# Key sums as a row of the key-value product, the first router from transposed rows, early queries, and output tiles moved off GpSimd in a two-layer attention kernel

## The chip, the cores and the metric

The kernel runs on one core of one Trainium2 chip. The metric is the device time of one execution in microseconds (us), median over several runs. Runs come in two states: a run is called slow when it is over 1.5% above the fastest of the same kernel. Ratios compare fast runs alone. The engines are TensorE (PE, its weight loads PEld), VectorE (DVE), ScalarE (ACT), GpSimd (POOL) and SyncE (SP). `SPq` and `ACTq` in the profile are the places from which these engines issue transfers.

## The reference

```python
def _A_ref(x, wqkv, wo):                       # S=2048, D=512, 32 heads of 16
    qkv = (x @ wqkv).reshape(B, S, 3, H, Dh).transpose(2, 0, 3, 1, 4)
    q, k, v = qkv[0], qkv[1], qkv[2]
    phi = lambda t: jnp.where(t > 0, t + 1, jnp.exp(t)) + 1e-6
    pq, pk = phi(q), phi(k)
    kv = einsum("bhsd,bhse->bhde", pk, v)
    z = einsum("bhsd->bhd", pk)                # the key sums
    num = einsum("bhqd,bhde->bhqe", pq, kv)
    den = einsum("bhqd,bhd->bhq", pq, z)[..., None] + 1e-6
    return (num / den).transpose(0, 2, 1, 3).reshape(B, S, D) @ wo
def _B_ref(x, w_r, w_gate, w_up, w_down):      # F=1376
    r = x @ w_r                                # the router
    idx = argsort(-r)[:, :2]                   # the two best rows of 2048
    x_sel = take(x, idx)
    y = (silu(x_sel @ w_gate) * (x_sel @ w_up)) @ w_down
    return x + scatter(idx, y * sigmoid(r[idx]))
for _ in range(2):
    x = x + _A_ref(_layernorm(x), A_wqkv, A_wo)
    x = x + _B_ref(_layernorm(x), B_w_r, B_w_gate, B_w_up, B_w_down)
```

## The kernel before

Rows lie in 16 tiles of 128. Layer normalization gives `xn`, a transfer transposes it to `xnT`. `K` makes the key features `pk` of a tile, `G` adds the tile to `pk^T xn` (four banks), `Q` makes query features. The value projection is applied to the product afterwards (`kv`). `den` makes the denominators, `O` the outputs of a tile. Every operation is entered in a list with its reads, writes and estimated duration; a list scheduler in the program then fixes each engine's order before the run. An edit in one place can therefore change the order everywhere behind it.

```python
def G(t, Gs, first=False, last=False):                # one tile's share of pk^T xn
    for c in range(NC):
        T_.matmul(Gs[c]()[:], lhsT=xn[:, t, c*P:(c+1)*P], rhs=pk[:, t, :], start=first, stop=last)

def z_piece(layer, zt, t, after=()):                  # key sums: 4 matmuls of one column per tile
    for c in range(NC):
        T_.matmul(zt()[:, c:c+1], lhsT=pk[:, t, c*P:(c+1)*P], rhs=ones_b[:], ...)

def r0_piece(t):                                      # router of layer 1's rows, in the same bank `zr`
    for c in range(NC):
        T_.matmul(zr()[:, NC+t:NC+t+1], lhsT=xnT[:, c, t*P:(t+1)*P], rhs=wr[:, c, :], ...)

def kv(layer, Gs):
    for i in range(NC):
        copy_ps(i, 0.5, GT[:, i, :], Gs[i], ("GT", i))         # two copies on ACT, two on DVE
    ...                                               # V weights x GT, block mask, output weights
# ... cut: layer 1's router is r0 plus a term from layer 1's queries; the two selected rows go
#     through gate, up and down, are normalized again (xc4) and patched into xnT ...
for i, t in enumerate(ORD[NT-k2-2:]):                 # only behind that patch:
    G(t, G2); z_piece(1, zr2, t, (1,))
    if i < QC: Q(i)                                   # the queries of layer 2
# ... cut ...
OUTK = [["POOL"]*4, ["POOL"]*4, ["ACT","DVE","ACT","DVE"], ["DVE","ACT","DVE","ACT"]]
# groups 0 and 1: scaled and stored during the output stage; 2 and 3: beside the last router
def store(lo, hi):                                    # 4 tiles, 512 KB
    nc.sync.dma_start(out=out_dram[:, lo:hi, :], in_=xo[:, lo:hi, :])
# ... cut: second router, gate, up, down of the two rows -> yo ...
# the two final rows, written over rows of the stored tiles, so behind all four stores:
e.dma_start(out=out_rows[:, ds(i, 1), :], in_=yo[...])         # one row on SP, one on ACT
```

Of the kernel before, what the change touches and what calls it, by code (L numbers as in the profile page):

```python
# [10 lines left out]
I32 = mybir.dt.int32  # L11
# [12 lines left out]
NR = 6  # L24
EPS = 1e-5
# [135 lines left out]
def linear_attention_moe(  # L161
# [95 lines left out]
    ones_b = big.tile([P, 1], BF16, name="ones_b")  # L257
    nc.vector.memset(ones_b[:], 1.0)
# [8 lines left out]
    sgnb = big.tile([4, 1], BF16, name="sgnb")  # L267
# [9 lines left out]
    xn = big.tile([P, NT, D], BF16, name="xn")  # L277
    xnT = big.tile([P, NC, S], BF16, name="xnT")
    pk = big.tile([P, NT, D], BF16, name="pk")
    pqT = big.tile([P, NJ, NC, D], BF16, name="pqT")  # L280
# [9 lines left out]
    r0 = big.tile([P, NT], FP32, name="r0")  # L290
    sd = big.tile([P, NT], FP32, name="sd")
    rr = big.tile([P, 2, NT], FP32, name="rr")
# [3 lines left out]
    KWr = [big.tile([P, NC, 2], BF16, name=f"KWr{i}") for i in range(2)]  # L296
# [20 lines left out]
    def tiny(fns, r, w, dur=0.07, **k):  # L317
        for f in fns:
            dve(dur, f, r=r, w=w, **k)
# [31 lines left out]
    def norm(kind, t, s_, b_, r, **k):  # L351
        if kind == "ACT":
            act(0.7, lambda: A.activation(out=xn[:, t, :], in_=x[:, t, :], func=ACT.Identity, scale=s_, bias=b_),
                r=[("x", t)] + r, w=[("xn", t)], **k)
        else:
            e = V if kind == "DVE" else G_

            def f():
                e.tensor_scalar(  # L359
                    out=xn[:, t, :], in0=x[:, t, :], scalar1=s_, scalar2=b_, op0=ALU.mult, op1=ALU.add  # L360
                )
            op(kind, 0.33 if kind == "DVE" else 0.76, f, r=[("x", t)] + r, w=[("xn", t)], port=True, **k)

    def trans(t, **k):
        def f():
            nc.sync.dma_start_transpose(out=xnT[:, :, t * P : (t + 1) * P], in_=xn[:, t, :])
        op("SP", 1.3, f, r=[("xn", t)], w=[("xnT", t)], lat=1.35, **k)
# [54 lines left out]

    def G(t, Gs, first=False, last=False, **k):
        def f():
            for c in range(NC):
                T_.matmul(  # L426
                    Gs[c]()[:], lhsT=xn[:, t, c * P : (c + 1) * P], rhs=pk[:, t, :], start=first, stop=last
# [6 lines left out]
    def Q(n, **k):  # L434
# [9 lines left out]
        phi(p, pqT[:, j, c, :], ("pq", j, c), relu=n < RQ[layer2[0]], **k)  # L444

    def z_mask(layer, zc, ap, r):
        zcs = small([P, NC, 1])

        def g():
            V.tensor_copy(out=zcs[:], in_=ap())  # L450
            V.tensor_tensor(
                out=Zs[layer][:], in0=headmask[:].to_broadcast([P, NC, 32]), in1=zcs[:].to_broadcast([P, NC, 32]),
                op=ALU.mult,
            )
        dve(0.3, g, r=r + ["masks"], w=["Z"])

    zr = ps("tp", [P, NC + NT])

    def z_piece(layer, zt, t, after=()):
        first = not after  # L460

        def f():
            for c in range(NC):
                T_.matmul(  # L464
                    zt()[:, c : c + 1], lhsT=pk[:, t, c * P : (c + 1) * P], rhs=ones_b[:],
                    start=first and c == 0, stop=layer == 0 and t == NT - 1, skip_group_check=True,
                )
        pl.lazy = 6.0
        pe(0.11, f, r=[("pk", t), zt] + (["zf%d" % layer] if after else ([("nmr", 2)] if layer == 0 else [])),
           w=[("z", layer, t)] + ([] if after else ["zf%d" % layer])).st = 0.01  # L470
        pl.lazy = 0.0

    def r0_piece(t):
        def f():
            for c in range(NC):
                T_.matmul(
                    zr()[:, NC + t : NC + t + 1], lhsT=xnT[:, c, t * P : (t + 1) * P], rhs=wr[:, c, :],
                    start=False, stop=(c == NC - 1), skip_group_check=True,
                )
        pl.lazy = 6.0  # L480
        pe(0.11, f, r=[("xnT", t), "wr", zr, "zf0"], w=[("r0p", t)]).st = 0.01
        pl.lazy = 0.0
# [7 lines left out]
    def kv(layer, Gs):  # L490
        for i in range(NC):
            copy_ps(i, 0.5, GT[:, i, :], Gs[i], ("GT", i))
        p = ps("g")
# [11 lines left out]
        pe(0.93, f, r=[("GT", i) for i in range(NC)] + ["wv"], w=[p])  # L505
# [4 lines left out]
        for c in range(NC):  # L510
            kw_one(layer, c)
        kr = ps("tp", [P, NC, 2])
# [11 lines left out]
        def h():  # L524
            V.tensor_reduce(out=krs[:], in_=kr()[:], axis=AX.X, op=ALU.add)
            split2(KWr[layer][:], krs[:])
# [18 lines left out]
    def den(layer, j, **k):  # L545
        p, ld, rb, sp, rd = ps("tp", [P, P]), sb("ld", [P, P], FP32), sb("rb", [P, P]), ps("mm", [P, NC, P]), sb("rd", [P, 1, D])

        def f():
            for c in range(NC):
                for g in range(NC):  # L550
                    T_.matmul(
                        p()[32 * g : 32 * (g + 1), :], lhsT=Zs[layer][:, c, :], rhs=pqT[:, j, c, g * P : (g + 1) * P],
# [19 lines left out]
        for c in (0, 2):  # L572
            q = pqT[:, j, c : c + 2, :]
# [4 lines left out]
    def O(layer, t, **k):  # L578
# [6 lines left out]
        def f(a, n):  # L585
            for c in range(NC):
                T_.matmul(  # L587
                    p()[:, a : a + n], lhsT=pqT[:, j, c, tt * P : (tt + 1) * P], rhs=KWs[layer][:, c, a : a + n],
# [37 lines left out]
    def lin(layer, lo, hi, tag="mm"):  # L626
# [3 lines left out]
        def f():  # L630
            for t in ts:
                j, tt = divmod(t, NJ)
                for c in range(NC):
                    T_.matmul(
                        p()[:, t - lo, :], lhsT=pqT[:, j, c, tt * P : (tt + 1) * P], rhs=KWr[layer][:, c, :],
# [4 lines left out]
        fs = [lambda: V.tensor_reduce(out=a[:], in_=p()[:], axis=AX.X, op=ALU.add)]  # L640
        if layer == 0:
            fs.append(lambda: V.tensor_tensor(out=rr[:, 0, lo:hi], in0=r0[:, lo:hi], in1=a[:], op=ALU.add))
        else:
            tiny([lambda: V.tensor_tensor(out=o[:], in0=rr[:, 0, lo:hi], in1=opr[:, 0, lo:hi], op=ALU.mult)],
                 r=["rrp"], w=[("ro", lo)])
            fs.append(lambda: V.tensor_tensor(out=rr[:, 1, lo:hi], in0=o[:], in1=a[:], op=ALU.add))
        tiny(fs, r=[p, "r0"] + ([("ro", lo)] if layer else []), w=[("rr", layer, lo)])
        tiny([
            lambda: V.scalar_tensor_tensor(
                out=rc[:], in0=mv[:, layer + 1, lo:hi, 0], scalar=nwr[:], in1=rr[:, layer, lo:hi],  # L650
                op0=ALU.mult, op1=ALU.add,
            ),
        ], r=[("rr", layer, lo), "nwr"] + [(f"mean{layer + 1}", t) for t in ts], w=[("rc", layer, lo)])
        tiny([
            lambda: V.tensor_tensor(
                out=key_hi(layer)[:, lo:hi], in0=rc[:], in1=rho[:, layer + 1, lo:hi], op=ALU.mult
            ),
        ], r=[("rc", layer, lo), "keys"] + [(f"rho{layer + 1}", t) for t in ts], w=[("key", layer, lo)])
# [4 lines left out]
    def mid_chain(lo, hi, kinds):  # L663
# [18 lines left out]
        ], r=w, w=[("s3", t) for t in ts])  # L682
        for t, kind in zip(ts, kinds):
# [16 lines left out]
    def consts_gp2():  # L700
# [7 lines left out]
        for sg in (sgn, sgnb):  # L708
            G_.memset(sg[:], 1.0)
            G_.affine_select(  # L710
                out=sg[:], in_=sg[:], compare_op=ALU.is_ge, fill=-1.0,
                base=-2, pattern=[[0, 1]], channel_multiplier=1,
            )

    def consts():
        pool(3.6, consts_gp, w=["masks0", "masks"])
        pool(1.3, consts_gp2, w=["pid", "rid"])
# [32 lines left out]

    def r0_all():
        def g():
            V.reciprocal(out=sd[:], in_=rho[:, 0, :])
            V.tensor_tensor(out=r0[:], in0=sd[:], in1=zr()[:, NC:], op=ALU.mult)
            V.tensor_scalar(
                out=sd[:], in0=mv[:, 0, :, 0], scalar1=nwr[:], scalar2=-1.0, op0=ALU.mult, op1=ALU.mult
            )
# [679 lines left out]
```

## Time and profile before

| | us |
|---|---|
| median of 3 runs | 171.97 (171.87 to 172.0) |
| span of the profiled execution | 170.1 |
| TensorE busy / VectorE busy | 154.0 / 133.2 |

The shares of busy time, the stages and the end are shown in the prediction below. The timeline shows the start, the duration, the engine, the line, output and inputs, and how many neighbouring instructions were merged. This is TensorE in layer 1's output stage:

```profile
54.99 0.41 PE L551 MATMUL tp<-pqT,Z 128*32 128x128 bf16 x16
...
59.48 2.75 PE L587 MATMUL g<-KW,pqT 128*128 128x512 bf16 x12
```

The first denominators begin at 54.99 and the first outputs at 59.48.

### The profile page before, as it was taken

The page shows a single profiled execution, that of the slowest core. Times are in us where ns is not written, and L with a number is a line of the kernel's source. Part 1 is how long each engine was busy: PE and PEld are TensorE (multiplying, and loading weights), DVE is VectorE, ACT ScalarE, POOL GpSimd, SP SyncE. Part 2 cuts the span into 40 slices and gives each one's busy share as a digit, 9 for nine tenths or more (in the row PEclk, how much of TensorE's full clock was granted, in tenths as well). Part 3 has the DMA queues.
Part 4 walks back from the last instruction along what each step waited for, and adds up shares of the span by engine and source line. Part 5 has one row for each costly group of instructions (what it writes and reads, how often), then busy time and mean ns, then how long its engine had stood idle before and what let it go on. Part 6 is the DMA issues. An engine that isn't in the chain of part 4 may idle for free.

```text
span 170.1 us, 4133 instructions
## 1 busy us (share of the span) xinstructions
PE 154.0 (91%) x1509; PEld 81.7 (48%) x1531; DVE 133.2 (78%) x483; ACT 106.7 (63%) x258; POOL 21.6 (13%) x52
## 2 busy tenths in 40 slices
PE   6989999999999999987999999999999999963771
PEld 2344544444465445542445565634446455443670
DVE  1499997867688899998968865637877999999640
ACT  3268967463544858899858223338899988795700
POOL 7321124000000000302030200000000000715000
PEclk9999999999999999999999999999999999998555
DMA  5997444599970000072423510000000000031530
GB/s 158 314 362 184 98 93 93 149 257 373 419 315 7 0 4 0 2 94 47 109 62 69 92 35 4 0 0 4 0 0 4 0 0 6 0 123 70 181 123 6
DMA packets 23589, 16.40 MB, mean 96 GB/s; under 512 B 17936, under 2 KB 21776, under 8 KB 23184
## 3 DMA queue, kind: packets, MB, share of 16 engines
q1 hardware_dynamic: 23272, 15.61, 31.7%
q10 hardware_dynamic: 296, 0.53, 0.9%
q8 instruction: 12, 0.20, 0.5%
q14 instruction: 9, 0.07, 0.2%
HBM read 9.83 MB, written 2.10 MB: 70 GB/s over the span
## 4 chain that ended last, share of the span: by engine, by line
PE 54%; DVE 31%; DMA 7%; issue 4%; SPq 1%; ACT 1%; DVEq 0%
PE mm L440 14%; PE g L426 13%; PE mm L402 12%; DVE x L596 9%; DVE pqT L574 5%; DMA xnT<-xn 5%; DVE st L325 3%; DMA x<-in_A_x_dram 3%; PE g L587 2%; PE g L979 1%; DVE em L375 1%; PE tp L979 1%; SPq L216 1%; PE g L499 1%; DVE pqT L382 1%
## 5 line engine op out<-in xcount | busy, mean ns | idle before, releaser
L371 ACT ACTIVATE e<-mm 128x512 bf16<-128x512 f32 x58 | 34.6, 601 | 29.7 <-PE mm L440 14.6
L440 PE MATMUL mm<-xnT,wq 128*128 128x512 bf16 x120 | 31.1, 379 | 0.7 <-DVE pqT L382 0.3
L426 PE MATMUL g<-pk,xn 128*128 128x512 bf16 x124 | 31.3, 379 | 0.3
L587 PE MATMUL g<-KW,pqT 128*128 128x512 bf16 (+1 forms) x127 | 29.3, 372 | 0.3
L402 PE MATMUL mm<-wk,xnT 128*128 128x512 bf16 x100 | 25.5, 379 | 2.4 <-DMA xnT<-xn 1.4
L375 DVE TENSOR_SCALAR em<-e 128x512 bf16<-128x512 bf16 x58 | 17.2, 302 | 11.9 <-ACT e L371 11.7
L604 ACT ACTIVATE sq<-x 128x512 bf16<-128x512 bf16 (+1 forms) x33 | 20.2, 611 | 4.4 <-DVE x L596 3.6
L587 PEld LDWEIGHTS <-pqT 128*128 128x128 bf16 x132 | 12.2, 97 | 12.6
L382 DVE SCALAR_TENSOR_TENSOR pk<-mm,em 128x512 bf16<-128x512 f32 x26 | 17.7, 685 | 0.4
L426 PEld LDWEIGHTS <-xn 128*128 128x128 bf16 x128 | 11.8, 98 | 12.4
L440 PEld LDWEIGHTS <-wq 128*128 128x128 bf16 x128 | 11.3, 97 | 12.5 <-issue 1.2
L402 PEld LDWEIGHTS <-xnT 128*128 128x128 bf16 x104 | 9.5, 97 | 13.3 <-DMA xnT<-xn 3.2
L325 DVE BATCH_NORM_STATS2 st<-x 128x6 f32<-128x512 bf16 x16 | 10.7, 683 | 5.0 <-DMA x<-in_A_x_dram 5.0
L596 DVE SCALAR_TENSOR_TENSOR x<-x,opr,g 128x512 bf16<-128x512 bf16 (+1 forms) x17 | 11.9, 707 | 0.0
L596 DVE SCALAR_TENSOR_TENSOR x<-x,g 128x512 bf16<-128x512 bf16 x16 | 10.6, 681 | 1.0 <-PE g L587 0.8
L382 DVE SCALAR_TENSOR_TENSOR pqT<-mm,em 128x512 bf16<-128x512 f32 x16 | 11.0, 689 | 0.4
L359 POOL TENSOR_SCALAR xn<-x,s,nb 128x512 bf16<-128x512 bf16 x5 | 4.1, 821 | 53.3 <-DVE mv L620 41.8
L1232 POOL TENSOR_SCALAR pk<-x,opr,nb 128x512 bf16<-128x512 bf16 x8 | 6.1, 772 | 37.3 <-DVE nb L1220 37.3
L574 DVE TENSOR_TENSOR pqT<-pqT,rd 128x1024 bf16<-128x1024 bf16 x16 | 10.5, 684 | 0.1
L374 ACT ACTIVATE rl<-mm 128x512 bf16<-128x512 f32 x16 | 9.8, 613 | 0.0
L339 ACT ACTIVATE lnv<-mv,eps_t 128x2 f32<-128x2 f32 (+2 forms) x18 | 5.1, 292 | 7.4 <-DVE mv L326 4.4
L464 PEld LDWEIGHTS <-pk 128*128 128x128 bf16 x128 | 5.8, 96 | 4.1
(238 smaller groups left out, 227.3 us busy)
## 6 DMA issues: line engine op xcount, KB each, us to landing
wgu<-in_B_wgu_dram SPq DMA_DIRECT2D x2, 1408.0 KB, 12.4
out_dram<-pk SPq DMA_DIRECT2D x4, 512.0 KB, 2.8
wd<-in_B_wd_dram SPq DMA_DIRECT2D x1, 1408.0 KB, 15.2
x<-in_A_x_dram SPq DMA_DIRECT2D x2, 512.0 KB, 5.6
xt<-in_A_xt_dram SPq DMA_DIRECT2D x3, 256.0 KB, 4.9
x<-in_A_x_dram SPq DMA_DIRECT2D x3, 256.0 KB, 4.8
wk<-in_A_wk_dram ACTq DMA_DIRECT2D x2, 256.0 KB, 4.0
wq<-in_A_wq_dram SPq DMA_DIRECT2D x1, 512.0 KB, 6.9
```

The costliest lines, as they stand in the source:

```text
L325: dve(0.61, lambda: V.bn_stats(out=st()[:], in_=x[:, t, :]), r=[("x", t)], w=[st]).early = 4.0
L371: act(0.5, lambda: A.activation(out=e()[:], in_=p()[:], func=ACT.Exp), r=[p], w=[e], **k)
L374: act(0.5, lambda: A.activation(out=rl()[:], in_=p()[:], func=ACT.Relu), r=[p], w=[rl], **k)
L375: dve(0.2, lambda: V.tensor_scalar(out=em()[:], in0=e()[:], scalar1=1.0, scalar2=TINY, op0=ALU.min, op1=ALU.add), r=[e], w=[em], port=True ...
L382: dve(0.6, lambda: V.scalar_tensor_tensor(out=out_ap, in0=p()[:], scalar=0.0, in1=em()[:], op0=ALU.max, op1=ALU.add), r=[p, em], w=[key], **k)
L402: T_.matmul(p()[:], lhsT=xnT[:, c, t * P : (t + 1) * P], rhs=wk[:, c, :], start=(c == 0), stop=(c == NC - 1))
L426: T_.matmul(Gs[c]()[:], lhsT=xn[:, t, c * P : (c + 1) * P], rhs=pk[:, t, :], start=first, stop=last)
L440: T_.matmul(p()[:], lhsT=wq[:, i, c, :], rhs=xnT[:, i, j * D : (j + 1) * D], start=(i == 0), stop=(i == NC - 1))
L574: dve(0.6, lambda q=q: V.tensor_tensor(out=q, in0=q, in1=rd()[:].to_broadcast([P, 2, D]), op=ALU.mult), r=[rd], w=[("pq", j, c), ("pq", j, ...
L587: T_.matmul(p()[:, a : a + n], lhsT=pqT[:, j, c, tt * P : (tt + 1) * P], rhs=KWs[layer][:, c, a : a + n], start=(c == 0), stop=(c == NC - 1),)
L596: dve(0.04 + 0.6 * n / D, lambda a=a, n=n: V.scalar_tensor_tensor(out=x[:, t, a : a + n], in0=x[:, t, a : a + n], scalar=1.0 if i == 1 els ...
L604: act(0.1 + 0.5 * n / D, lambda a=a, n=n, sq=sq: A.activation(out=sq()[:, 0:n], in_=x[:, t, a : a + n], func=ACT.Square, scale=float(D) ** ...
```

## The change

Its intent: take small matmuls off TensorE (the key sums come out as one more row of a product that is made anyway), free a bank early, start layer 2's queries before the router's result is known and patch two of them afterwards, and shorten the end by keeping POOL out of it.

```diff
+    nc.gpsimd.memset(xn[:, :, D : D + 1], 1.0)            # ones column; rows are now 544 wide
+    def gcol(c):
+        return c * P + (c == NC - 1)                      # last slice starts one element later
-    lhsT=xn[:, t, c * P : (c + 1) * P]
+    lhsT=xn[:, t, gcol(c) : gcol(c) + P]
-    (z_piece, z_mask, r0_piece, r0_all: removed)
+    def center():                                         # a normalized row sums to 0, so the dropped
+        ... V.tensor_tensor(out=wv, in0=wv, in1=wl, op=subtract)   # column is restored through wv
     def kv(layer, Gs):
-        for i in range(NC):
+        for i in (3, 2, 1, 0):
             copy_ps(i, 0.5, GT[:, i, :], Gs[i], ("GT", i))
+        zf: 4 matmuls take the key sums from GT's last row
-            lin(0, t - 3, t + 1)                          # first router from layer 1's queries
+            logits(t - 3, t + 1)                          # from the transposed rows of layer 2
     for i, t in enumerate(ORD[NT - k2 - 2 :]):            # moved: now ahead of the patch of xnT
         G(t, G2)
         if i < QC: Q(i)                                   # QC 7 -> 8
+    pqx: 16 matmuls, 3 small operations and 2 copies replace the two queries' features
-    OUTK = [["POOL"]*4, ["POOL"]*4, ["ACT","DVE","ACT","DVE"], ["DVE","ACT","DVE","ACT"]]
+    OUTK = [["POOL"]*4, ["ACT","DVE"]*2, ["ACT","DVE"]*2, ["DVE","ACT","DVE","DVE"]]
-    (groups 0 and 1 scaled and stored in the output stage)
+    (group 0 only; groups 1 to 3: one set of scales and all tiles beside the last router)
... (cut: bookkeeping of the two query tiles, gates of the output tiles, table load)
```

## The prediction

> **What bounds the kernel now.** I read the shares of busy time, then the same by stage, then TensorE's timeline, then the timeline of the end.
>
> ```profile
> PE 154.0 (91%) x1509; PEld 81.7 (48%) x1531; DVE 133.2 (78%) x483; ACT 106.7 (63%) x258; POOL 21.6 (13%) x52
> ...
> PE 54%; DVE 31%; DMA 7%; issue 4%; SPq 1%; ACT 1%; DVEq 0%
> ```
>
> TensorE (PE) leads in busy time and in the chain that ended last, VectorE (DVE) is second. The shares hide stages, so I cut the span where the program changes its work: layer 1's keys and products; its key-value product; its outputs; layer 2's keys with the routed-token work beside them; layer 2's key-value product and outputs; the end.
>
> ```profile
> core 0: us, PE busy (x) PEld busy (x) DVE busy (x) ACT busy (x) POOL busy (x), PEclk, DMA share, GB/s
> 21.60:48.50 26.90, 26.71 (x175) 12.90 (x179) 21.21 (x53) 14.45 (x28) 2.80 (x5) 1.00 0.76 246
> 48.50:59.50 11.00, 10.25 (x175) 6.17 (x175) 9.15 (x23) 6.63 (x14) 0.00 (x0) 1.00 0.14 57
> 59.50:78.40 18.90, 16.84 (x168) 8.55 (x168) 18.43 (x78) 14.99 (x48) 1.52 (x2) 1.00 0.20 29
> 78.40:127.30 48.90, 48.33 (x426) 24.73 (x433) 35.30 (x134) 28.78 (x67) 4.19 (x7) 1.00 0.17 34
> 127.30:153.30 26.00, 23.87 (x261) 13.09 (x263) 24.57 (x90) 23.18 (x65) 3.76 (x5) 1.00 0.06 22
> 153.30:170.10 16.80, 8.59 (x210) 7.50 (x210) 8.93 (x52) 5.67 (x13) 2.29 (x4) 0.58 0.27 96
> ```
>
> PE is full in the first and fourth stage; DVE is full in the third (18.43 of 18.90) and nearly so in the fifth (24.57 of 26.00); the last is a chain of small steps, with the clock at 0.58. Since ends of matmuls are modelled, I checked PE by starts: a group of four 512-column matmuls starts every 0.86 us (0.2155 each) almost without a hole from 21.6 to 151. The holes I find are some 0.4 and 0.7 us near 50 and 57, 0.9 at 73 and 1.3 at 77 (waits for transposes).
>
> ```profile
> 18.84 0.44 PE L464 MATMUL tp<-ones_b,pk 128*128 128x1 bf16 x12
> 19.15 0.54 PE L476 MATMUL tp<-wr,xnT 128*128 128x1 bf16 x16
> ```
>
> Twelve key-sum matmuls hold PE from 18.84 to 19.15: 26 ns each, though each shows 164 ns long. That is the price of a small matmul here.
>
> ```profile
> 152.56 3.03 POOL L1232 TENSOR_SCALAR pk<-x,opr,nb 128x512 bf16<-128x512 bf16 x4 [3.90 <-DVE nb L1220]
> 153.59 0.52 DVE L1218 TENSOR_SCALAR opr<-rho 128x4 f32<-128x4 f32 x1
> 154.20 0.65 DVE L1220 TENSOR_TENSOR nb<-rho 128x4 f32<-128x4 f32 x1
> 154.96 0.64 DVE L621 SCALAR_TENSOR_TENSOR mv<-mv 128x4 f32<-128x4 f32 x1
> 155.83 0.30 ACT L339 ACTIVATE lnv<-mv,eps_t 128x4 f32<-128x4 f32 x1 [1.89 <-DVE mv L623]
> 158.24 1.23 PE L910 MATMUL tp<-identf,s 128*128 128x128 f32 x4 [0.26 <-DVE s L1284]
> ```
>
> Right after the last output, DVE's tiny operations take 0.52 to 0.65 us instead of some 0.16, exactly while GpSimd (POOL) writes four output tiles. They stand in front of the last row sums, so they hold up the final router.
>
> **What the Trainium skill says.** "TensorE: Matmul & The Clock Gate", section "Wait — 56ns, not 53.3ns?": start to start never falls below about 25 ns, however few columns; the trace has 26. "Perfetto Trace Analysis", section "Identifying the Most-Contended Engine": matmul busy time doesn't show how near TensorE is to its limit; the trace agrees (0.38 us shown, 0.2155 between starts). "Advanced Engine Details and Errata", section "Mode Summary": GpSimd and two-port VectorE instructions block each other over a shared port; the slow tiny operations above fit, though one of them is of a kind that its table doesn't give two ports. "VectorE: DVE Perf Modes", section "The perf-mode tier table": a bf16 tensor-tensor runs at twice the base rate, 1224 ns for 2048 elements; the trace has 684 ns for 1024, which fits.
>
> **The change, part by part.**
>
> *Small matmuls.* Removed: 128 + 4 key sums (32 tiles by 4, and the correction), 64 router pieces on layer 1's rows, 64 on layer 1's queries, 16 for their weights: 276. Added: 8 that take the key sums out of the product's last row, 64 router pieces on layer 2's rows, 16 for two corrected query columns: 88, and one 512-column matmul. The built order has 187 matmuls fewer, which agrees. At 26 ns: 188 x 0.026 - 0.22 = 4.7 us of PE (a little less, since the 16 run side by side). By stage it is worth less:
> - Before 21.6: 28 go (0.7 us), ahead of a wait for a transpose: nothing gained.
> - 21.6 to 48.5: 40 key sums, 1.0 us, less 0.2 for the new matmul. But the weights must have one row subtracted first: one DVE operation on 128x2048, an estimate of 1.2 us at the 1024-element rate (two of these back to back take 1.28 with the pipeline overlap). The order puts it directly ahead of DVE's two copies of the product, which the key-value matmuls await. Before, these copies ran 46.66 to 47.94 and the matmuls began at 48.46; now about 47.0 to 48.3. **Gain about 0.**
> - 48.5 to 78.4: 48 router pieces held the only bank of their pool until the 0.8 us of DVE router arithmetic at 54.9, and the first denominators waited for it (PE at 54.99, outputs from 59.48). Now key sums, denominators, value matmuls and two more denominators follow at once. In the new order, from 48.45: 0.9 + 0.86 + 0.1 + 0.86 + 0.35 + 0.9 + 0.35 + 0.86 + 0.2 + 0.86 + 0.2 = 6.4, so outputs from 54.9, with two query groups (1.7 us) more left to do: PE is 2.9 us ahead. DVE binds here, so it decides: idle of 1.9 us before 59.5, mostly removed; 0.8 (router), 0.4 (router weights), about 1.0 (key arithmetic of three groups) saved; 0.6 (reciprocals brought forward) and about 1 us of pushed-back work added. **Gain 2.3 us.**
> - 78.4 to 127.3: removed 68 key sums and 16 others, 2.2 us; added 64 + 16, 2.1 us; a query group and a denominator (1.2 us) move behind the key-value product, which is no gain. **Gain about 0.4 us.**
>
> *Router later, queries earlier.* Layer 1's router now needs the last transposed rows: its gather stands behind all 26 key groups, before behind 18. From there the corrected tokens need at least (durations of before): 0.6 broadcast, 0.6 top two, 0.4 index, 1.6 register load, 1.3 copy, 0.5 select, 0.2 scale, 2.4 gate and up, 1.3 activation, 1.2 down, 0.5, 0.15, 1.8 normalization: 12.6 us. PE has 14.4 us of ordered work in that time (5 query groups, 6 product groups, the chain's own matmuls), since queries no longer wait and two columns are patched afterwards. So PE should stay full, with perhaps 0.4 us lost at the selection. That is what "begun early" is for: it pays for the later router rather than saving by itself.
>
> *127.3 to 153.3.* DVE gets one query's tail more (0.55) and the key-sum mask (0.4), loses two groups of output scales (0.35) and GpSimd's interference there. **About 0.**
>
> *The end.* GpSimd writes 4 tiles instead of 8, early; the scales of 12 tiles are one group after the top-8. So the last row sums finish right after ACT's last square (153.94): about 154.3 for ACT's logarithm against 155.83. The early top-two moves ahead too: its gather ends near 156.0 instead of 158.0, and the last broadcast starts near 156.4 against 158.24. Then three output tiles (3 x 0.37) stand on DVE before the final gate and cost perhaps 0.2. **Gain 1.7 us.** The table load moved behind two output tiles; ACT had 3.6 us of slack there, so it is free.
>
> Sum: 0 + 2.3 + 0.4 + 0 + 1.7 = 4.4 us, and I add 0.4 for holes at 73 to 78 that earlier rows may close: 172.0 - 4.8 = **167.2 us**.
>
> **Rivals.** (a) *PE counts in full*: all 4.7 us leave the path and the end too, about 165. For it: PE is full for 100 us. Against it: DVE is as full in 45 of these. (b) *The later router becomes the bound*: DVE takes each step behind 0.6 to 0.7 us query and key tails, PE stands, and 2 to 4 us go: 169 to 171. For it: before, the chain took 21.5 us from broadcast (89.97) to corrected tokens (111.68), much of it queueing. Against it: the 12.6 us above. (c) *DVE gets slower*: a query row of 1026 elements, or products that start one element off, could take a slower mode. The 16 scalings of 0.68 us at half the rate would add some 8 us. Against it: starts stay multiples of 4 bytes, sizes are equal. I give it 4%. (d) *The output stage is DVE's alone*, so all that came earlier is lost there, leaving the end's gain: 170. Against it: its work starts when the key-value product is done, and that comes earlier.
>
> **Range and chances.** Stage two is the widest term (0.5 to 3.5), then the router (0 to -3), then the end (1 to 2). Range 165.0 to 170.0. Over 2% faster is below 168.5: 0.71; within 2%: 0.26; slower: 0.03.
>
> **What would show it.** Small matmuls: one-column key sums gone, 26 ns for the rest. Key-value product still near 48.5 (right if DVE's subtraction ends near 47.0). Outputs of layer 1 from about 55; layer 2's first keys near 71.8. Broadcast of the first router near 99 to 100, PE without holes over 0.5 us behind it, layer 2's key-value product near 123. Last output near 150.5 to 149, the last DVE sums at 0.16 us each, last broadcast 3 us behind the last output instead of 4.9. It would be wrong if PE shows holes in the router's stage, if DVE's scalings leave 0.68 us, or if the last stores delay the end.

## More of the kernel before

The view of SyncE's waits lists who waited for what: total us, number of waits, longest.

```profile
SPq L1378 <- DVE yo L1374: 3.2, 1, 3.2
...
SPq L1378 <- DMA out_dram<-pk: 1.4, 1, 1.4
```

L1378 issues a final row. It found the tile stores (`out_dram<-pk`) done after a wait of 1.4 us and then waited another 3.2 us for `yo`, the tile with the two final rows: the stores had 3.2 us to spare.

## The result, and the profile after

The changed kernel took 167.72 us (median of 4 runs, 167.45 to 168.37), the kernel before 171.99 beside it (4 runs, 171.87 to 172.35). The ratio is 0.9754, 95% interval 0.972 to 0.9787: faster. Ratios here are the mean time of one kernel's fast runs over that of the other's of the same rounds, so not quite the ratio of the medians quoted.

The shares of busy time and the chain that ended last, after:

```profile
PE 149.3 (90%) x1326; PEld 77.2 (46%) x1344; DVE 132.9 (80%) x481; ACT 107.1 (64%) x261; POOL 19.0 (11%) x52
...
PE 53%; DVE 27%; DMA 8%; issue 5%; ACT 2%; SPq 1%; DVEq 0%
```

TensorE has 183 matmuls fewer in the trace and 4.7 us less to do; DVE's time is the same. In the stages (columns as in the prediction's table, boundaries set by eye), the three in the middle read:

```profile
59.50:76.00 16.50, 15.84 (x114) 7.32 (x108) 16.36 (x62) 14.97 (x47) 2.29 (x3) 1.00 0.17 33
76.00:124.00 48.00, 46.45 (x420) 24.41 (x429) 36.80 (x151) 27.84 (x65) 3.63 (x9) 1.00 0.20 35
124.00:150.00 26.00, 24.18 (x264) 13.06 (x268) 24.28 (x92) 23.07 (x66) 3.02 (x4) 1.00 0.07 22
```

The lengths of these windows are not gains: 59.5 is the same instant as in the prediction's table but not the same point of the program, since the first outputs now begin at 55.48. The starts of operations (table below) show where time was won. From the key-value product of layer 1 to its first outputs it is 6.86 us instead of 11.02, with the first denominators at 51.37 instead of 54.99. From the first outputs to the first keys of layer 2 it is 15.04 instead of 14.63, with DVE full in most of it (16.36 of 16.50), and from these to the first outputs of layer 2 60.30 instead of 60.08. The last window, from 150.0, is 16.7 us long; the prediction's, from 153.3, is 16.8. That looks as if the new end had brought nothing. The timeline of the end says otherwise:

```profile
150.78 0.30 ACT L343 ACTIVATE lnv<-mv,eps_t 128x4 f32<-128x4 f32 x1 [0.70 <-DVE mv L608]
...
151.91 0.17 DVE L1229 TENSOR_TENSOR nb<-rho 128x12 f32<-128x12 f32 x1
...
157.92 1.40 SPq L1246 DMA_DIRECT2D out_dram<-pk  x1
...
160.56 0.29 DVE L1384 CAST yo<-g 128x128 bf16<-128x128 f32 x1 [1.47 <-PE g L1372]
163.41 0.73 SPq L1388 DMA_DIRECT2D out_dram<-yo  x1
163.42 1.14 ACTq L1388 DMA_DIRECT2D out_dram<-yo  x1
```

The small DVE operation `nb<-rho` takes 0.17 us where it took 0.65, and the logarithm (`lnv`) comes at 150.78, 5.05 us earlier than before (155.83). `yo` is ready at 160.85, against 166.83: **5.98 us earlier**. But the two final rows, which went out 0.03 us after `yo` before, now go out at 163.41, **2.56 us after it**. The waits of SyncE name the reason, and the list of transfers gives the time from issue to landing:

```profile
SPq L1388 <- DMA out_dram<-pk: 2.8, 3, 1.3
```

```profile
out_dram<-pk SPq DMA_DIRECT2D x4, 512.0 KB, 4.7
```

The rows wait for the tile stores. Three of the four stores are now issued between 155.77 and 157.92 and take 4.64 to 5.33 us to land (4.7 is the median of all four); before, two were issued at 159.22 and 160.63 and landed in 2.8 and 2.9. In the two microseconds in which they end, the transfers look like this (last two columns: share of the 16 DMA engines busy, GB/s):

```profile
161.00:162.00 1.00, 0.00 (x0) 0.00 (x0) 0.00 (x0) 0.00 (x0) 0.00 (x0) 0.50 0.50 172
162.00:163.00 1.00, 0.00 (x0) 0.00 (x0) 0.00 (x0) 0.00 (x0) 0.00 (x0) 0.50 0.06 22
```

A share of 0.06 is one engine of 16. Cut finer, that engine moves 25 GB/s from 161.75 to 162.75 while the other fifteen are idle. The Trainium skill ("DMA: Bandwidth & Descriptors", section "Why a DMA increments its semaphore by 16 and not by 1") says that a transfer's engines finish independently and that only all of them together mean that it has landed; this trace agrees, and shows a price of some 1.3 us.

To see where time was won and lost I use the starts of seven marks in the program; times between marks can be subtracted.

| mark (start, us) | before | after | e10 (key sums only) | e6 (no early queries) | e3 (old end) | e8 (store order) |
|---|---|---|---|---|---|---|
| key-value product, layer 1, in full flow | 48.46 | 48.62 | 49.28 | 48.37 | 48.24 | 48.18 |
| first outputs of layer 1 | 59.48 | 55.48 | 58.32 | 55.23 | 55.10 | 55.04 |
| first keys of layer 2 | 74.11 | 70.52 | 73.46 | 70.27 | 70.14 | 70.08 |
| first outputs of layer 2 | 134.19 | 130.82 | 132.49 | 133.82 | 130.46 | 130.47 |
| last residual addition | 152.86 | 149.01 | 150.90 | 151.71 | 148.98 | 148.65 |
| `yo` | 166.54 | 160.56 | 165.32 | 164.00 | 162.77 | 159.85 |
| row store issued | 166.86 | 163.41 | 165.64 | 166.43 | 163.09 | 161.01 |

From before to after: 3.37 us are won by the first outputs of layer 2, 0.48 in the output stage, 2.13 from there to `yo`; 2.53 are given back between `yo` and the row store. That leaves 3.45 us in these two executions. The row store stands for the time: the span ends 3.2 to 3.4 us after it in every profile here but e6 (3.7). The profile after is of the slowest of its four runs (span 166.7, the others 165.7 to 166.2); the wait is 2.1 us in e6 and 2.4 in e7 (a slow profile), which have the same end, so 2.5 need not be its typical size.

### The profile page after: what moved, and what is told of

The parts are those of the page before. It is cut to its first block, busy times and chain, and to the rows that moved or that the text cites. A ratio compares the mean times of both kernels' runs of the same rounds, so it can differ in the third digit from the quotient of the medians.

```text
span 166.7 us, 3771 instructions
## 1 busy us (share of the span) xinstructions
PE 149.3 (90%) x1326; PEld 77.2 (46%) x1344; DVE 132.9 (80%) x481; ACT 107.1 (64%) x261; POOL 19.0 (11%) x52
## 4 chain that ended last, share of the span: by engine, by line
PE 53%; DVE 27%; DMA 8%; issue 5%; ACT 2%; SPq 1%; DVEq 0%
PE g L433 13%; PE mm L447 13%; PE mm L406 10%; DVE x L581 6%; DMA xnT<-xn 5%; PE g L572 5%; DVE st L329 4%; DVE pq L559 3%; DMA x<-in_A_x_dram 3%; PE tp L977 1%; DVE pq L386 1%; PE g L482 1%; SPq L218 1%; PE g L519 1%; PE tp L536 1%
## 5 line engine op out<-in xcount | busy, mean ns | idle before, releaser
L447 PE MATMUL mm<-xnT,wq 128*128 128x512 bf16 x121 | 31.8, 379 | 0.6 <-DVE pq L386 0.2
L572 PE MATMUL g<-KW,pq 128*128 128x512 bf16 (+1 forms) x129 | 29.8, 373 | 0.2
L572 PEld LDWEIGHTS <-pq 128*128 128x128 bf16 x132 | 12.3, 98 | 13.8 <-DVE pq L559 0.6
L386 DVE SCALAR_TENSOR_TENSOR pq<-mm,em 128x512 bf16<-128x512 f32 x16 | 11.0, 687 | 0.3
L559 DVE TENSOR_TENSOR pq<-pq,rd 128x1024 bf16<-128x1024 bf16 x16 | 10.4, 683 | 0.5 <-ACT rd L554 0.5
L383 DVE TENSOR_TENSOR pq<-rl,em 128x512 bf16<-128x512 bf16 x16 | 6.6, 420 | 0.9 <-ACT rl L378 0.7
L363 POOL TENSOR_SCALAR xn<-x,rho,nb 128x512 bf16<-128x512 bf16 x6 | 4.6, 770 | 17.5 <-DVE nb L351 14.3
```

The costliest lines, as they stand in the source:

```text
L386: dve(0.6, lambda: V.scalar_tensor_tensor(out=out_ap, in0=p()[:], scalar=0.0, in1=em()[:], op0=ALU.max, op1=ALU.add), r=[p, em], w=[key], **k)
L447: T_.matmul(p()[:], lhsT=wq[:, i, c, :], rhs=xnT[:, i, j * D : (j + 1) * D], start=(i == 0), stop=(i == NC - 1))
L559: dve(0.6, lambda q=q: V.tensor_tensor(out=q, in0=q, in1=rd()[:].to_broadcast([P, 2, D]), op=ALU.mult), r=[rd], w=[("pq", j, c), ("pq", j, ...
L572: T_.matmul(p()[:, a : a + n], lhsT=pqt(c, t * P, P), rhs=KWs[layer][:, c, a : a + n], start=(c == 0), stop=(c == NC - 1),)
```

## The experiments

My theory after reading both traces: the early part was won around layer 1's first outputs; early queries only hold what would be lost to the later router; the new end wins about 2 us and gives it back in the wait for the stores. The main rival: the store wait only looks like one, because the program's end waits for the same stores anyway. Each run was timed against the kernel before on the same chip. Of one kernel's runs, some are up to 2.2 us longer than others in the same state. Two of the profiled executions below (e2_g1_pool, e4_new_tail) show where such a difference can arise: they are 1.2 and 1.5 us late already near 22 us. I therefore read positions as differences between marks.

### Is the wait for the stores real?

**e1_scratch**: the final rows go to a spare tensor (two rows of the output are wrong).

```diff
-    out_rows = out.flatten_outer_dims().rearrange("s (o d) -> o s d", o=1)
+    scr = nc.dram_tensor("scr", (S, D), BF16, kind="Internal").ap()
+    out_rows = scr.rearrange("s (o d) -> o s d", o=1)
-    act(0.1, f, r=["yo"] + [("out", lo) for lo in range(0, NT, NJ)])
+    act(0.1, f, r=["yo"])
```

> The changed kernel with its two final row stores sent to a spare tensor in device memory, so that nothing makes them wait for the four tile stores (two output rows are wrong on purpose). Theory A (the row stores were held by the tile stores): they are issued within 0.2 us of the end of the last copy (yo, about 160.9 us in the profile) instead of 2.56 us after it, the span falls from 166.7 to 164.2 and the median from 167.7 to about 165.3. Rival B (the wait only looks like one, and the end of the program waits for the same tile stores in any case): the row stores go out early but the median stays between 167.2 and 168.0.

Measured: 165.68 us, the median of three fast runs (165.15 to 167.33; a fourth, 167.63, is slow, and with it the median is 166.51), ratio 0.9673 (0.9596 to 0.975), against 0.9754 with the wait. In the timeline of this run:

```profile
160.31 0.29 DVE L1385 CAST yo<-g 128x128 bf16<-128x128 f32 x1 [1.47 <-PE g L1373]
160.62 0.73 SPq L1389 DMA_DIRECT2D scr<-yo  x1
```

The rows go out 0.02 us after `yo` ends, 2.8 us earlier than in the changed kernel, and the profiled span is 164.0 us against 166.7. Theory A holds in the trace: the rows no longer wait, and the span ends as much earlier. In the medians of fast runs the gain is 2.0 us, by the ratios 1.4, with runs that differ by more than that among themselves and intervals that overlap.

**e1b_scratch_before**: the same edit in the kernel before, as a control.

> The same edit in the kernel before (two rows wrong on purpose), as the control. Theory A: there the last tile store had landed about 3 us before yo was ready, so the median stays within 0.3 us of 172.0. If it falls by 1 us or more, the edit itself saves something and the neighbouring run proves less.

Measured: 171.69 us (4 runs), ratio 0.9995 (0.997 to 1.0021). The edit itself saves nothing; there was no wait to take away.

### Is POOL the reason that the end is shorter now?

**e2_g1_pool**: the second group of output tiles on POOL in the output stage again, and stored there.

```diff
-    OUTK = [["POOL"] * 4, ["ACT", "DVE"] * 2, ...
+    OUTK = [["POOL"] * 4, ["POOL"] * 4, ...
-            if i < 4:                      # groups scaled and stored in the output stage
+            if i < 8:
-    last_scales(4, NT, ["k8"])
+    last_scales(8, NT, ["k8"])
-    for g in (1, 2, 3):
+    for g in (2, 3):
```

> The changed kernel with the second group of four output tiles scaled during the output stage on POOL, as before the change, and stored then. Theory A: with two stores instead of three left for the last 10 us, the row stores wait at most 0.5 us; yo itself comes up to 1 us later than 160.9 because POOL runs beside the small DVE operations again; median 165.7 to 166.7. Rival B (the wait is not what costs): 167.7 or, with POOL's contention, 168 to 169.

Measured: 169.47 us (4 runs, 168.75 to 170.48), ratio 0.9854 (0.9799 to 0.9908): slower than the changed kernel by about 1.7 us, outside what Theory A gave and above Rival B with POOL's contention. Its timeline:

```profile
150.38 3.03 POOL L1241 TENSOR_SCALAR pk<-x,opr,nb 128x512 bf16<-128x512 bf16 x4 [3.40 <-DVE nb L1229]
...
151.99 0.68 DVE L605 TENSOR_SCALAR mv<-sums 128x4 f32<-128x4 f32 x1
...
152.75 0.66 DVE L606 SCALAR_TENSOR_TENSOR mv<-mv 128x4 f32<-128x4 f32 x1
...
154.57 0.30 ACT L343 ACTIVATE lnv<-mv,eps_t 128x4 f32<-128x4 f32 x1 [3.21 <-DVE mv L608]
```

Four operations on POOL, and the same small DVE operations take 0.68 and 0.66 us instead of 0.14 to 0.17. From the last residual addition (150.27) to `yo` (163.93) it takes 13.66 us: the 13.68 of before, where the changed kernel takes 11.55. The next run has the same early group without POOL and takes 12.01 us there (149.02 to 161.03), so POOL's neighbourhood is most of what the new end saves up to `yo`. The 1.7 us of the median are not its price: the profiled run was 1.2 us late near 22 us already, and two of the four runs are some 1.5 us above the other two (168.75 and 168.78). From the last residual addition to the row store it takes 14.94 us, against 14.40 in the changed kernel, because the rows waited only 1.0 us for the stores.

**e2_g1_split**: the same, but the group goes to ACT and DVE by turns (the edit as above with `["ACT", "DVE"] * 2` kept, and the gate of the output tiles beginning at group 2).

> The changed kernel with the second group scaled during the output stage on ACT and DVE by turns, and stored then. Theory A: row stores wait at most 0.5 us, no POOL contention; but four more operations (2 of 0.4 us on DVE, 2 of 0.8 us on ACT) lie in the output stage, where DVE is busy 93%: last output 0 to 0.8 us later than 149.5; median 165.3 to 166.5. Rival B: 167.7 to 168.5.

Measured: 167.52 us (4 runs, 167.11 to 169.25), ratio 0.9781 (0.9725 to 0.9837): no gain that can be told from the changed kernel. In the trace `yo` comes at 161.03 (0.47 later) and the row store at 162.16 (1.25 earlier): the wait fell from 2.56 to 0.84 us and not to below 0.5. The last store still went out at 158.41, which I put down to the scheduler: the table load waits for the last group's ACT tile, so that tile is done ahead of the earlier groups'.

### What is the new end worth, with the wait?

**e3_old_tail**: the changed kernel with the whole end of the kernel before.

```diff
-    OUTK = [["POOL"]*4, ["ACT","DVE"]*2, ["ACT","DVE"]*2, ["DVE","ACT","DVE","DVE"]]
+    OUTK = [["POOL"]*4, ["POOL"]*4, ["ACT","DVE"]*2, ["DVE","ACT"]*2]
... (cut: scales by group, gates and table load as before)
```

> The changed kernel with the whole end of the kernel before: two groups of output tiles on POOL during the output stage, scales by group, ACT tiles behind the table load. Theory A (the new end gains about 2 us up to yo and gives about 2.5 back in the wait for the tile stores): no wait of the row stores, yo 13.5 us after the end of the last residual addition as before instead of 11.4, so the span is near 166.3 and the median 167.3 (166.7 to 168.5), within 1 us of the changed kernel. Rival B (the term of 1.7 us for the end stands, nothing is given back): 169.4.

Measured: 168.06 us (4 runs, 167.87 to 168.44), ratio 0.9783 (0.976 to 0.9807), within Theory A. From the last residual addition to `yo` it takes 13.79 us (11.55 with the new end); counted from the end of that addition, as in the expectation, 13.6 to the end of `yo`, and the rows go out 0.03 us after `yo`. So the row store comes at 163.09, even 0.3 us earlier than in the changed kernel. The new end wins 2.2 us up to `yo` and all of it is given back to the stores; with the rest of the change in place it moves the time by some half a microsecond (ratios 0.9783 and 0.9754), within the intervals.

**e4_new_tail**: the kernel before with the new end only.

> The kernel before with nothing changed but the end (kinds of the output tiles, one set of scales, gates, table load, priorities of the tiny operations). Theory A: yo is ready about 2 us earlier (164.7 instead of 166.8), but the row stores are issued 13.9 us after the end of the last residual addition, as in the changed kernel, at about 167.3 instead of 166.9: median 172.0 to 172.8. Rival B: 170.3, and no wait of the row stores above 0.5 us.

Measured: 171.13 us (4 runs, 170.36 to 172.22), ratio 0.9943 (0.9903 to 0.9983): between the two expectations. The profile fell on the slowest of these runs, which was 1.5 us late before 23 us. From the last residual addition to `yo` it has 12.12 us instead of 13.68, and the rows then wait 0.47 us for the stores. The shortening is there, and the wait is smaller than I expected, because the stores landed in 2.8 to 3.2 us here and in up to 5.3 in the changed kernel (see e11_store_spread). From the last residual addition to the row store it takes 12.88 us instead of 14.00: in the kernel before, the new end wins 1.1 us. The two runs at 170.36 and 170.60 agree with that, if the two others owe their distance to the early delay; the median alone is inconclusive about the size.

### Can the wait be taken away correctly?

**e8_store_order**: all ACT tiles ahead of the table load, the last group shared two and two, three DVE tiles free to go ahead of `xs`.

```diff
-    r.append({..., "DVE": "k8" if t < ORD[8] else "xs"}[kind])
+    r.append({..., "DVE": "k8" if t < ORD[10] else "xs"}[kind])
-    OUTK = [..., ["DVE", "ACT", "DVE", "DVE"]]
+    OUTK = [..., ["ACT", "DVE"] * 2]
-    act(1.3, ..., r=[("xo", ORD[13])], w=["table"])
+    act(1.3, ..., r=[("xo", ORD[i]) for i in range(4, NT) if OUTK[i // 4][i % 4] == "ACT"], w=["table"])
```

> The changed kernel with all six ACT output tiles ahead of the table load, in the order of their groups, the last group shared two and two, and three DVE tiles allowed ahead of xs: each group is complete, and stored, earlier (first of the three stores near 153.5 instead of 155.8, last near 157.2 instead of 157.9). Theory A: row stores wait at most 0.7 us after yo (161.0), span near 164.5, median 165.3 to 166.5. Rival B (the transfers end at the same time whatever the order): 167.3 to 168.0.

Measured: 166.58 us (4 runs, 165.84 to 167.22), ratio 0.9702 (0.9658 to 0.9746), correct. The three stores go out at 153.31, 154.72 and 156.46. Its timeline:

```profile
156.46 0.37 SPq L1246 DMA_DIRECT2D out_dram<-pk  x1
...
159.85 0.29 DVE L1384 CAST yo<-g 128x128 bf16<-128x128 f32 x1 [1.47 <-PE g L1372]
161.01 0.73 SPq L1388 DMA_DIRECT2D out_dram<-yo  x1
```

`yo` ends at 160.14 and the rows wait 0.87 us, not 2.56; the row store is 2.4 us earlier than in the changed kernel, of which 0.35 were there by the first outputs of layer 2. Theory A holds, with a little more wait left than expected: the last store needed over 4 us, and again one DMA engine alone was busy (25 GB/s from 159.0 to 160.5).

**e11_store_spread**: in addition the second group early, as in e2_g1_split (and the gate of the DVE tiles moved with it), so that the four stores lie apart.

> The run e8_store_order with the second group scaled and stored during the output stage, on ACT and DVE, so that the four stores lie apart (near 146, 151, 154 and 156.3) and no more than two can overlap. Theory A (back-to-back stores are what makes the last one land late, and one of the 16 DMA engines finish after the others): the longest landing of a tile store falls from 4.9 us to at most 3.6, DMA traffic ends with no stretch of 25 GB/s behind it, and the row stores go out within 0.4 us of yo; yo itself 0.3 to 0.8 us later than in e8_store_order, because four operations stand in front of the last sums; median 166.0 to 166.9. Rival B (a late landing belongs to any store next to the final computation): landing 4.4 or more, row stores held 0.5 us or more, median 166.8 to 167.6.

Measured: 166.60 us (6 runs, 165.89 to 168.06), ratio 0.9699 (0.9657 to 0.9741), correct. The stores went out at 145.39, 150.74, 153.77 and 156.27; the rows go out 0.03 us after `yo` (160.63 to 160.92). `yo` is 0.78 us later than in e8_store_order, so the row store is at the same place (160.95 against 161.01). The longest landing fell to 4.0 us, not to 3.6, and DMA still ends with about 1 us of 16 to 23 GB/s (159.0 to 160.0).

Close stores are not the reason by themselves. The times to landing in the changed kernel and in e4_new_tail (min, median, max of the four stores):

```profile
DMA to landing us min/median/max: 3.7/4.7/5.3
DMA to landing us min/median/max: 2.8/2.9/3.2
```

e4_new_tail has three stores as close together (issued at 161.34, 162.84 and 163.88), and they land in 2.90, 2.79 and 3.23 us; the changed kernel's, at 155.77, 157.28 and 157.92, in 4.85, 4.64 and 5.33. The first store of each run lies alone. In its best half microsecond it moves at 387 GB/s in the three profiles that have nothing of the change but at most the end (before, e1b, e4), and at 334 to 352 in the eleven others, e10 among them. e3_old_tail, with the old end, also has landings of up to 4.4 us. So the late landings come with the earlier parts of the change, and not with the new end. By an estimate, with e4's longest landing (3.23 us) the changed kernel's last store would have landed at 161.15, 0.3 us after `yo`. Which part does it is not shown: e10, with the key sums alone, has the lower rate, but its stores land in 2.9 to 3.0 us without a lone engine at the end.

### What do early queries pay for?

**e6_queries_late**: the queries of layer 2 behind the patch of `xnT` again, their own patch removed.

```diff
-    for i, t in enumerate(ORD[NT - k2 - 2 :]):     # moved back behind the patch
-        G(t, G2)
-        if i < QC: Q(i)
-    qp, qe, pqx = ...                              # and the patch of two queries removed
```

> The changed kernel with the queries of layer 2 begun only once the repaired rows stand in the transposed input, as in the kernel before; their own repair is gone with it. Theory A: the eight query groups of 0.86 us (6.9 us) that TensorE now does before the repair at 114 us leave holes there; about 2.9 us of key-value work that now lies behind it can fill them, and 0.54 us of repair matmuls are saved: median 170 to 171.5. Rival B (the router's chain alone sets the time and TensorE has other work): 167.4 to 168.4.

Measured: 171.83 us (4 runs, 171.65 to 171.91), ratio 0.9995 (0.9975 to 1.0014), just above Theory A: the whole gain of the change is gone. First keys of layer 2 still come at 70.27, but the first outputs at 133.82, 3.0 us later than in the changed kernel. One part of it I had not expected. In this run seven product matmuls that start at 105.73 take 2.94 us to the next instruction instead of 1.51 (7 x 0.2155), and the granted clock reads 0.50 from 106 to 109. It is not a wait but a slower TensorE; why the clock fell is not shown (the changed kernel has the same 88 small matmuls ahead of it, at 105.20, and stays at 1.00). All runs of this kernel show a low mean clock (0.941 to 0.952; the changed kernel 0.954 to 0.963). Of the 3.0 us, 1.4 are that. Most of the rest is TensorE standing still: between the first keys and the first outputs of layer 2 it is idle for 3.87 us, against 2.17 in the changed kernel. The medians do not hang on the clock alone: the run with 0.952, which by an estimate had no such drop (3 us at 0.50 lower the mean of 170 us by 0.009), still took 171.65. The edit moves key products back together with the queries, so the two are not told apart.

### What are the key sums worth by themselves?

**e10_keysum_only**: the kernel before with the ones column, the rolled and reduced weights and the key sums from the product, and nothing else (`center` takes a bank of another pool, since the router pieces still hold theirs).

> The kernel before with only the first part of the change: ones column, key sums from the key-value product, rolled and reduced V weights. Router, queries and end as before. Theory A (the 1.0 us of key-sum matmuls ahead of the product is eaten by the 1.23 us subtraction, and the later 1.9 us lies where the router's chain sets the time): product at 48.5, first keys of layer 2 at 74.1, both within 0.5 us of before; median 171.3 to 172.4. Rival B (TensorE time taken away counts in full, some 3 us): 169.0 to 170.0.

Measured: 170.50 us (4 runs, 170.35 to 170.78), ratio 0.9901 (0.9862 to 0.9939), correct. Its timeline on TensorE:

```profile
49.28 1.05 PE L491 MATMUL g<-GT,wv 128*128 128x128 bf16 x16
...
58.32 3.62 PE L579 MATMUL g<-KW,pqT 128*128 128x512 bf16 x16
```

Theory A fell. The product starts even 0.8 us later than before (the scheduler put 40 router pieces, 1.0 us, directly ahead of it, at 48.28; before, they followed it), yet the first outputs come 1.2 us earlier, the first outputs of layer 2 1.7 us earlier, and the time falls by about 1.7 us (0.99% of 172). Rival B (3 us) did not hold either: the gain is about half of the removed TensorE time (132 key sums less 8 small matmuls, 124 x 0.026 = 3.2 us). Most of what was won by the first keys of layer 2 comes with the router's new source: these keys of layer 2 come 0.65 us earlier in this run and 3.59 in the changed kernel, so 2.9 us belong to the router, or to the two together.

### Is the subtraction from the V weights on the path?

In the changed kernel the timelines of DVE and TensorE show the order that the prediction foresaw:

```profile
46.14 1.23 DVE L720 TENSOR_TENSOR wv<-wv,e 128x2048 bf16<-128x2048 bf16 x1
47.28 1.28 DVE L457 CAST GT<-g 128x512 bf16<-128x512 f32 x2
```

```profile
48.62 1.00 PE L482 MATMUL g<-GT,wv 128*128 128x128 bf16 x15 [0.59 <-DVE GT L457]
...
55.48 3.79 PE L572 MATMUL g<-KW,pq 128*128 128x512 bf16 x16
```

**e7_no_center**: the subtraction left out (wrong result).

```diff
-    center()
-    pe(0.93, f, r=[("GT", i) for i in range(NC)] + ["wvc"], w=[p])
+    pe(0.93, f, r=[("GT", i) for i in range(NC)] + ["wv"], w=[p])
```

> The changed kernel with the subtraction from the V weights left out (wrong result on purpose): the cost of that subtraction by itself. Theory A (the 0.8 us hole in front of the product is on the path): product in full flow at 47.7 instead of 48.6, first keys of layer 2 0.5 to 0.9 us earlier than 70.5, median 166.8 to 167.3. Rival B (the output stage of layer 1 is bound by DVE and takes it up): first keys within 0.3 us of 70.5, median 167.5 to 168.0.

Measured: 168.60 us median of 5 runs, the four fast ones 168.11 to 168.73, ratio of the fast runs 0.978 (0.9741 to 0.9818): no faster than with the subtraction (0.9754), above both expectations and nearer to Rival B. The only profile was slow (span 169.2), so I take the positions from the next run, which agrees with it up to the outputs of layer 1.

**e9_combo**: e8_store_order, and the subtraction moved some 7 us forward, in four pieces of 128x512.

```diff
+            if t == 12: center()                   # in the loop over layer 1's tiles
-    consts()
-    center()
+    consts()
... (cut: four subtractions instead of one, the mask for it made first)
```

> The changed kernel with the stores in the order of their groups (as in the run e8_store_order) and the subtraction moved some 7 us forward, in four pieces, among the last keys and queries of layer 1. Theory A (DVE has 0.6 us of slack in each 2.6 us there, so most of the 1.3 us is hidden): product at 47.7 to 48.0, row stores issued near 160.3, median 165.7 to 166.3. Rival B (DVE feeds TensorE there and the four pieces stop it as long as the one did later): as e8_store_order, 166.3 to 167.0.

Measured: 166.85 us (4 runs, 166.46 to 167.06), ratio 0.9692 (0.9655 to 0.9729), correct; e8_store_order without the move has 0.9702, as Rival B said. On TensorE:

```profile
47.61 1.06 PE L482 MATMUL g<-GT,wv 128*128 128x128 bf16 x16
...
56.47 3.62 PE L572 MATMUL g<-KW,pq 128*128 128x512 bf16 x16
```

The product starts 1.0 us earlier than in the changed kernel, and the first outputs 1.0 us *later*. Between them the scheduler chose another order: the third group of denominators and one more query group stand in front of the outputs on TensorE, and four query scalings in a row in front of the first residual additions on DVE. By the row store (161.50 against 161.01) nothing is won. So the subtraction does set the start of the product, as the prediction said; but the orders that the scheduler made of the earlier start (here and in e7) won nothing by the end.

## Why the prediction was right or wrong

The time was right (167.72 measured, 167.2 predicted), partly by luck, because two errors had opposite signs: the computation came out 1.2 us better than the sum of 4.8 (5.98 us up to `yo`), and the stores took back 2.5 that the sum didn't contain.

- *Small matmuls at 26 ns, and the places.* Right: one-column key sums are gone, 16 router pieces take 0.40 us (97.48 to 97.88). Product at 48.62 (near 48.5), subtraction ended at 47.37 (47.0), outputs of layer 1 at 55.48 (55), router's broadcast at 99.61 (99 to 100), last broadcast 2.8 us behind the last output (3). The second product came at 121.97 instead of 123.
- *Counts.* The total of 276 is right, the list by stage is short: 28, 40, 48 and 84 make 200. The trace of before has 12 more key sums and the 64 router pieces on layer 1's queries between 48.5 and 78.4, and the 16 for their weights there too, not behind 78.4: 92 x 0.026 = 2.4 us that the term for that stage left out. The chain "from broadcast to corrected tokens" took 21.7 us by its own marks, not 21.5.
- *"Gain about 0" for the key sums ahead of the product.* The position was right, the reading of it wrong. The step took the product's start for what counts there. e10 has a later product (behind router pieces that had to be done anyway) and still a gain, e9 an earlier product and none. The key sums as a whole, which the sum credits with little on the path, measured about 1.7 us alone.
- *"Gain 2.3 us" for 48.5 to 78.4.* The mechanism fits the traces (denominators 3.6 us earlier, outputs 4.0), but no run frees the bank alone; in e10, which keeps the router pieces, the first denominators come at 52.30 and the outputs only at 58.32. The term, with the 0.4 added for holes, was too small: 3.59 us by the first keys of layer 2, of which 0.65 belong to key sums alone. The hole in front of layer 2's keys did not close but moved: 1.11 us at 82.91, after 1.17 at 77.27 before.
- *"Gain about 0.4 us" for 78.4 to 127.3, and early queries paying for the later router.* By the first outputs of layer 2 the gain had gone from 3.59 to 3.37: -0.2 instead of +0.4. That early queries (with the key products moved beside them) pay for the router is shown by e6: without them the gain is zero, 4.1 us by the medians. e6 shows a part of rival (b): TensorE stands for 1.99 us behind the router's broadcast, against 0.76 in the changed kernel; the clock and waits ahead of the broadcast make up the rest. With early queries TensorE has no hole over 0.5 us in the router's stage behind the broadcast.
- *Output stage "about 0".* 0.48 us were won; e3, with POOL back, has 0.33 of it lost again.
- *"Gain 1.7 us" for the end.* The mechanism was right (e2_g1_pool, e3) and the term a little small: 2.13 us up to `yo`. The step that failed is the one left out: the sum ended at `yo`. The last stores appear only as the final condition under which it would be wrong ("if the last stores delay the end"), with no number. They cost 2.5 us (e1, e3), so that in the changed kernel the net of the new end is nothing; in the kernel before it is 1.1 us (e4). The difference is that the same stores land later once the earlier parts of the change are in (up to 5.3 us against 3.2), which no term of the sum holds.
- *Rival (c), DVE slower on 1026-element rows or odd starts*: refuted, a scaling takes 683 ns (684 before), and four product matmuls, one of them with the odd start, still take 0.86 us from start to start (22.03 to 22.89; before, 22.51 to 23.37). *Rival (d)*: refuted, what was won by the start of the output stage (3.37 us) was still won at its end (3.85). *Rival (a)*, everything counts: the computation of the changed kernel gained more than all of TensorE's 4.7 us, but through other terms; e10 counts about half.

What stays open: which earlier part of the change makes the stores land later, with one DMA engine of 16 ending up to 1.5 us after the others; and how the scheduler's reordering, rather than the removed work, divides the gain of the first stages. e8, e9 and e11 all beat the kernel before by 3%; against the changed kernel their ratios are some 0.5% lower with overlapping intervals, and only the traces (row store 1.9 to 2.5 us earlier) show the cause.

## What to carry to other kernels

Follow the sum to the last transfer, not to the last computation: list when each store is issued and landed, and whether its slack is larger than what the change is going to win. A gain of six microseconds met a slack of three here. Compare the landing times of the same transfers before and after as well: a change elsewhere had made them longer. In a kernel whose order is made by a list scheduler, the start of one stage is a poor measure for the end; undo one part at a time and compare several marks.

## What the Trainium skill lacked or had wrong

- "TensorE: Matmul & The Clock Gate", section "Back-to-back issue gap", gives about 131 ns per matmul of 512 columns for sustained streams. Here four such matmuls with their weight loads start every 0.86 us at a granted clock of 1.00, 215.5 ns each, for over 100 us; the page's figure for a single matmul (about 216 ns) is the one that fits.
- "DMA: Bandwidth & Descriptors" says that a transfer's engines finish independently, but not how far apart. The same stores of 512 KB landed in 2.8 to 5.4 us here, the longest of them with a single engine at about 25 GB/s for the last 1.0 to 1.5 us.
- No page that I read says what weights that start at an odd element of a 544-element row cost in a matmul; here nothing (0.86 us from start to start for four matmuls of 512 columns, as before).
